# Pooled attention with four experts: a fourth expert's up-projection of the first chunk in seven products instead of eight

## The chip, the cores and the metric

The kernel runs on one core of a Trainium2 chip. A core has a matrix engine (TensorE, PE), a vector engine (VectorE, DVE), a scalar engine (ScalarE, ACT), GpSimd (POOL) and SyncE (SP), each with a queue of its own, and 16 DMA engines. Matrix products are written to PSUM[...]. The metric is the device time of one execution in microseconds (us), as a median of several runs.

## What is computed

Attention over pooled keys and values, and then four experts on every token, weighted by normalized probabilities. Cut to what matters:

```python
# q, k, v: (8 batches, 8 heads, 576 rows, 64)
k_p = k.reshape(B, H, 72, 8, D).mean(axis=3)
v_p = v.reshape(B, H, 72, 8, D).mean(axis=3)
attn = softmax(q @ k_p.T / 8)
x = (attn @ v_p).transpose(0, 2, 1, 3).reshape(4608, 512)
p = probs / (probs.sum(-1, keepdims=True) + 1e-9)      # (4608, 4)
for e in range(4):                                     # w1: 512x1024, w2: 1024x512
    out += p[:, e:e+1] * (relu(x @ w1[e]) @ w2[e])
```

## The kernel before, in words

**Chunks.** The 4608 tokens are worked on as nine chunks of 512: the first 512 rows of each batch (chunks 0 to 7), and the 64 remaining rows of all eight batches together (chunk 8). Each chunk goes through an up-projection (`up`, `up_product`) and a down-projection (`down`, `down_plain`) for each of the four experts. All weights stay in SBUF as bf16. `add` (L825, or L823 for expert 0) multiplies a down product by its probability and adds it to `acc`.

**Seven products.** A projection can be done plainly, or as a 2 x 2 block product with seven block products in place of eight (the Strassen-Winograd scheme). For the plain up-projection, `up` (L596) makes eight blocks of four products with 512 columns (L603), each followed by a relu on ScalarE (L608). For the seven-product one, `up_product` (L663) is called with a step 0 to 6 and a unit 0 or 1 (a unit is half of the hidden columns of each block). Each call makes four products of 256 columns (L681). A unit has two PSUM banks. Step 0 goes into bank 0 and ScalarE copies it into bank 1 (L694). Steps 2 and 3 are copied to the SBUF tile `partial` by ScalarE (L696), steps 1 and 5 end with a relu on ScalarE (L698, L702), and steps 4 and 6 with `relu_sum` on VectorE (L661), which adds a part of `partial`. Beside this the scheme needs sums of blocks: four weight differences for each expert (`first_weight_sums`, L631, the fourth in place in w1), four sums of x for each chunk (`x_sums`, L647), and for the down-projection `weight_sums` (L708) and `hidden_sums` (L721). All of these run on VectorE through `combine` (L245).

**Memory that is shared.** In chunk 0 the partial sums lie in the room of w2 of expert 3 (`partial_first`), so w2 of expert 3 is loaded (`load_w2(3)`, L215) only after their last reader. The x sums of chunk 0 lie in `x_rem`. The keys and values of batch 1 are loaded into `wt_bf`. The hidden rows of experts 0 and 3 of chunk 0 share a buffer.

**PSUM.** Two banks `att`, two banks of unit 1 (`units[1]`), two banks of down chains (`chains`, names `o_ps`), and two banks that are at first `att_first` and later unit 0 (`units[0]`, from the pool `psum_last`). `two_banks(b)` gives attention of batches 0 and 1 `att` and `att_first` in turn.

**The order.** Each engine's order is the program's order, written by hand. `attention_first` makes batch 0's attention and the first expert's up-projection. `first_chunk` (L852) is the rest of chunk 0, with batch 1's attention between its products: expert 1's up-projection plainly, expert 2's by seven products (`both`), expert 3's plainly; expert 0's down-projection by seven products, those of experts 1 and 2 plainly; expert 3's runs in the main loop. Batch 1's queries and keys are transposed on TensorE (`queries`, L356; `keys`, L299) and copied from PSUM by ScalarE or VectorE. `scores` (L374, exponential L385) and `scores_of_two` (exponential L398), `context` (L448), `divide` (L409, L410) and `turn` (L466) follow. Then comes the main loop: for each slot `g` unit 0 makes step `g % 7`, unit 1 makes the step before, and `down` makes a product of the chunk and expert before; a table of slots (`pieces_later`, L948) puts the attention of later batches, their loads and the x sums between the slots. From batch 2 on, transposes are done by DMA from SP's queue: `queries` at L347, `keys` at L293, `turn` at L462, and for the remaining rows of two batches `rem_queries` at L472. `rem_scores` (L485), at slot 6 for batches 0 and 1, reads what L472 delivers; its rows of q come through `load_q_rem` (L197). The loads go through POOL's queue in the order that they are called in.

Of the kernel before, what the change touches and what calls it, by code (L numbers as in the profile page):

```python
# [12 lines left out]
BF16 = mybir.dt.bfloat16  # L13
# [4 lines left out]
def kernel(  # L18
# [10 lines left out]
    nc = tc.nc  # L29
# [230 lines left out]
    def two_banks(b):  # L260
        return att_first[turn_of("att", 2)] if b < 2 else att

# [27 lines left out]
    def keys(b, hs):  # L290
        state[("kpT", b)] = kpTs[b % 3]
        if b >= BUSY:
            nc.sync.dma_start_transpose(  # L293
                out=state[("kpT", b)][:, 0:H], in_=kp_all[:].rearrange("j h a d -> j (h a d)")
            )
            return
        kpt_ps = one_bank(b).bitcast(BF16)[:, 0:H * SP].rearrange("p (h j) -> p h j", j=SP)
        for h in range(hs.start, hs.stop):
            nc.tensor.transpose(kpt_ps[:, h, :], kp_all[0:SP, h], ident[:SP, :SP])  # L299
        copy = nc.scalar.copy if b else nc.vector.tensor_copy  # L300
        copy(out=state[("kpT", b)][:, hs, 0:SP], in_=kpt_ps[:, hs])
# [28 lines left out]

    def open_bank(ps):

        nc.tensor.matmul(ps, lhsT=ident[:], rhs=w1_bf[:, 0, 0, 0:NT], skip_group_check=True)

    def values_folds(b):
# [6 lines left out]
    def queries(b, pair=0):  # L342
# [3 lines left out]
        if b >= BUSY:  # L346
# [4 lines left out]
            return  # L351
        bank = one_bank(b) if b else att_first[pair % 2][:, 0] if pair >= 2 else chains[(pair + 1) % 2][:]
        qt_ps = bank.bitcast(BF16)[:, 0:4 * P].rearrange("p (h a t) -> p h a t", h=2, a=2)
        for hh in range(2):
            for rr in range(2):
                nc.tensor.transpose(  # L356
                    qt_ps[:, hh, rr, :], q_sb[:, 2 * pair + hh, 2 * rr:2 * rr + 2, :], ident[:]
                )
        copy = nc.scalar.copy if pair in ((1, 3), (1, 2))[b] else nc.vector.tensor_copy
        copy(out=state[("qT", b)][:, 2 * pair:2 * pair + 2], in_=qt_ps)  # L360

    def key_columns(b, h, lo):
# [27 lines left out]

    def scores_of_two(b, pair):


        scores(b, pair, 0)
        banks = [unit[1][:] for unit in units]
        score_products(b, pair + 1, banks)
        for r2 in range(2):
            nc.scalar.activation(  # L398
                out=state[("expT", b)][:, 2 * pair + 2:2 * pair + 4, :, r2].rearrange("j h a t -> j (h a) t"),
                in_=banks[r2][0:SP].rearrange("j (h t) -> j h t", t=P),  # L400
                func=ACT.Exp, scale=EXP_SCALE,
            )
# [260 lines left out]
    def up_product(c, e, unit, step):  # L663
        b11, b21, t3, b22 = weight_parts(e)
        a11, _, a12, a22 = x_parts(c)
        t, s, s3 = wu_bf[:, e], state[("xs", c)], third_sum(c)
        banks = units[unit] or [att_first[1][:, i] for i in range(2)]
        bank, grows, lhs, rhs = [
# [183 lines left out]
    def first_chunk():  # L852
# [7 lines left out]

        def both(step):
            for unit in range(2):
                up_product(0, 2, unit, step)

# [6 lines left out]
        each(*sums[1][0:3])  # L871
        up(0, 1, (4,), bank=att_first[1][:, 1])
        each(sums[2][0], sums[2][1], sums[2][3], sums[2][2])
        up(0, 1, (5,), bank=chains[0])
        both(0)
        up(0, 1, (6,), bank=chains[1])
        both(1)
        up(0, 1, (7,), bank=chains[0])
        last_sum = weight_sums(0)
        each(sums[0][3], sums[1][3], *last_sum[0:2])  # L880
        both(2)
        down(0, 0, 0)
        both(3)
        hidden_sums(0, 0, 2)
        down(0, 0, 1)
        both(4)
        hidden_sums(0, 0, 3)
        down(0, 0, 2)
        both(5)
        each(*last_sum[2:])  # L890
        down(0, 0, 3)
        both(6)
        load_w2(3)
        up(0, 3, (0,), bank=units[1][0])
        down(0, 0, 4)
        sums[3][0]()
        fold_keys(1)
        up(0, 3, (1, 2, 3))
        down(0, 0, 5)
        sums[3][1]()  # L900
        down(0, 0, 6)
        up(0, 3, (4,))
        queries(1, 0)
        queries(1, 1)
        sums[3][2]()
        up(0, 3, (5,))
        keys(1, every)
        queries(1, 2)
        up(0, 3, (6,))
        queries(1, 3)  # L910
        up(0, 3, (7,))
        scores(1, 0)
        scores(1, 1)
        each(*weight_sums(1)[0:3])
        down_plain(0, 1, 0)
        fold_first, *fold_rest = values_folds(1)
        fold_first()
        scores(1, 2)
        scores(1, 3)
        each(*fold_rest)  # L920
# [24 lines left out]
        turn(1, 3)  # L945
        each(*(lambda n=n: x_sum(1, n) for n in range(4)))

    def pieces_later():  # L948


        at, amid = {}, {}

# [61 lines left out]
    with tc.manual_schedule(  # L1014
# [14 lines left out]
        load_w1(3)  # L1029
        attention_first()  # L1030
        load_whole(1, k, "kraw")
        load_q(1)
# [3 lines left out]
        first_chunk()  # L1036
        psum_first.__exit__(None, None, None)
        psum_last = ctx.enter_context(
            tc.tile_pool(name="psum_last", bufs=1, space=bass.MemoryType.PSUM))
        units[0] = [psum_last.tile([P, NT], F32, name=f"unit0{i}") for i in range(2)]  # L1040
        open_bank(units[0][1][:])


# [4 lines left out]
        sums = {}  # L1048
        for at, pieces in (((3,), weight_sums(3)[3:]), ((8,), weight_sums(1)[3:]), ((10, 15, 22, 14), weight_sums(2)),
                           ((15,), first_weight_sums(3)[3:])):  # L1050
            for slot, piece in zip(at, pieces, strict=True):
# [57 lines left out]
```

The softmax here doesn't subtract the row's maximum and nothing guards it: scores larger than these inputs give would overflow.

## Time and profile before

| | us |
|---|---|
| median of 4 runs | 491.67 |
| lowest, highest run | 491.49, 492.02 |
| profiled execution | 491.6 |
| its span, first to last instruction | 489.4 |
| TensorE busy in the span | 482.7 |
| VectorE busy | 376.8 |
| ScalarE busy | 304.8 |
| GpSimd busy | 116.5 |

The profile is one execution. Its times count from the span's start. A line of the timeline reads: start, duration, engine, source line, operation, written tile <- read tiles, shapes, number of merged instructions, and in brackets how long the engine stood idle and what ended this. PEld are the weight loads of TensorE, which run beside its products. POOL and SPq lines with DMA are issues; a transfer's landing is told separately, as us from issue to landing. Consecutive instructions on one engine overlap, so the time that an instruction takes of its engine is read from start to start: two `relu_sum`s of 0.69 and 0.68 us start at 40.27 and 40.88. In the stretch of the change the trace has these places: step 6 of expert 2's up-projection starts at 39.53 on TensorE, expert 3's up-projection runs from 40.41 to 51.21 among other work, expert 1's plain down products start at 51.76, chunk 1's first product starts at 66.66.

### The profile page before, as it was taken

Reading aid. Unit: us, or ns where it says so; the run is one execution under the profiler, and the core shown is the slowest. Engines: PE = TensorE matmul, PEld = TensorE weight load, DVE = VectorE, ACT = ScalarE, POOL = GpSimd, SP = SyncE. Lnnn points to the kernel's source line nnn. Section 1 sums busy time; section 2 is a strip of 40 time slices with the busy share of each in tenths; the row PEclk is TensorE's granted clock in tenths of the full one; section 3 lists DMA queues with packets and bytes.
Section 4 is the critical chain, followed back from the end, with each engine's and each line's share of the span. In section 5 each row is a group of like instructions: output and inputs, shape, how many; then the busy total and the mean of one; then the engine's idle time right before and its main releaser. Section 6 shows DMA issues by size and latency. Waiting matters only on the chain.

```text
span 489.4 us, 11551 instructions
## 1 busy us (share of the span) xinstructions
PE 482.7 (99%) x4701; PEld 410.5 (84%) x4701; DVE 376.8 (77%) x758; ACT 304.8 (62%) x580; POOL 116.5 (24%) x115
## 2 busy tenths in 40 slices
PE   8999999999999999999999999999999999999996
PEld 4867468898888888888898888888888888888885
DVE  5778799799768976798679866897678766876674
ACT  5776546855685567657665567556755566556650
POOL 8320323242423055015311452111011101010100
PEclk9999999999999999999999999999999999999999
DMA  9999999995986579544954297311111010004003
GB/s 199 209 208 204 201 165 139 105 85 65 100 118 57 85 81 136 40 79 54 164 49 90 26 160 72 68 23 65 35 23 23 23 66 2 13 21 87 1 1 87
DMA packets 101828, 41.97 MB, mean 86 GB/s; under 512 B 73856, under 2 KB 100224, under 8 KB 101776
## 3 DMA queue, kind: packets, MB, share of 16 engines
q0 software_dynamic: 56944, 22.42, 41.4%
q1 hardware_dynamic: 43728, 17.77, 16.6%
q10 hardware_dynamic: 1104, 1.05, 0.6%
q8 instruction: 37, 0.61, 0.5%
q14 instruction: 15, 0.12, 0.1%
HBM read 45.69 MB, written 9.44 MB: 113 GB/s over the span
## 4 chain that ended last, share of the span: by engine, by line
PE 96%; POOL 1%; DMA 1%; issue 0%; DVE 0%; POOLq 0%
PE o_ps L749 41%; PE unit L681 41%; PE o_ps L775 3%; PE unit L603 2%; PE att L448 1%; PE unit L808 1%; DMA wt_bf<-in_v_dram 1%; PE att L374 1%; PE o_ps L603 1%; POOL wt_bf L141 1%; PE unit L618 1%; PE att_first L681 1%; PE unit L374 0%; PE o_ps L618 0%; PE att L502 0%; PE att L485 0%
## 5 line engine op out<-in xcount | busy, mean ns | idle before, releaser
L825 DVE SCALAR_TENSOR_TENSOR acc<-o_ps,p_all,acc 128x256 f32<-128x256 f32 (+1 forms) x285 | 127.1, 487 | 52.6 <-PE o_ps L749 37.8
L749 PEld LDWEIGHTS <-H 128*128 128x128 bf16 x1320 | 129.1, 98 | 15.2
L681 PEld LDWEIGHTS <-w_bf 128*128 128x128 bf16 x1056 | 102.2, 98 | 12.7 <-issue 0.2
L661 DVE CUSTOM_DVE_ANT_0 H<-unit,partial 128x512 bf16<-128x512 f32 x128 | 87.4, 686 | 26.1 <-ACT partial L696 12.6
L749 PE MATMUL o_ps<-w_bf,H 128*128 128x256 bf16 x792 | 102.6, 273 | 0.0
L681 PE MATMUL unit<-xT,w_bf 128*128 128x256 bf16 x680 | 97.5, 273 | 0.0
L696 ACT COPY partial<-unit 128x512 f32<-128x512 f32 x128 | 72.4, 593 | 29.9 <-PE unit L681 29.9
L763 POOL TENSOR_TENSOR acc<-acc,addend 128x512 f32<-128x512 f32 x24 | 30.4, 1266 | 254.2 <-ACT addend L761 203.1
L681 PEld LDWEIGHTS <-wu_bf 128*128 128x128 bf16 x792 | 75.3, 98 | 11.4 <-issue 2.5
L681 PE MATMUL unit<-xs,wu_bf 128*128 128x256 bf16 x512 | 77.0, 273 | 0.0
L749 PE MATMUL o_ps<-wt_bf,H 128*128 128x256 bf16 x528 | 68.4, 273 | 0.0
L698 ACT ACTIVATE H<-unit 128x512 bf16<-128x512 f32 x64 | 38.9, 607 | 31.5 <-PE unit L681 31.5
L749 PEld LDWEIGHTS <-S 128*128 128x128 bf16 x528 | 51.7, 98 | 6.2
L702 ACT ACTIVATE H<-unit 128x512 bf16<-128x512 f32 x64 | 38.6, 603 | 25.8 <-PE unit L681 25.5
L694 ACT COPY unit<-unit 128x512 f32<-128x512 f32 x65 | 37.9, 584 | 22.0 <-PE unit L681 17.3
L681 PE MATMUL unit<-xs,w_bf 128*128 128x256 bf16 x256 | 38.4, 273 | 0.0
L823 ACT ACTIVATE acc<-o_ps,p_all 128x256 f32<-128x256 f32 x72 | 30.7, 486 | 10.3 <-PE o_ps L749 8.4
L151 POOL DMA_DIRECT2D kraw<-in_k_dram x20 | 26.4, 1320 | 40.7 <-DMA kraw<-in_k_dram 40.7
L681 PE MATMUL unit<-xT,wu_bf 128*128 128x256 bf16 x228 | 34.2, 272 | 0.0
L749 PE MATMUL o_ps<-wt_bf,S 128*128 128x256 bf16 x264 | 34.2, 273 | 0.0
L749 PE MATMUL o_ps<-w_bf,S 128*128 128x256 bf16 x264 | 34.2, 273 | 0.0
L151 POOL DMA_DIRECT2D vraw<-in_v_dram x20 | 29.2, 1462 | 18.5 <-DMA vraw<-in_v_dram 18.5
(170 smaller groups left out, 520.0 us busy)
## 6 DMA issues: line engine op xcount, KB each, us to landing
out_dram<-acc SPq DMA_DIRECT2D x32, 256.0 KB, 4.5
w_bf<-in_moe_w_dram POOLq DMA_DIRECT2D x6, 1024.0 KB, 20.9
q_sb<-in_q_dram POOLq DMA_DIRECT2D x7, 512.0 KB, 9.9
vraw<-in_v_dram POOLq DMA_DIRECT2D x22, 144.0 KB, 6.7
kraw<-in_k_dram POOLq DMA_DIRECT2D x21, 144.0 KB, 6.4
w_bf<-in_moe_w_dram POOLq DMA_DIRECT2D x4, 512.0 KB, 13.7
wt_bf<-in_k_dram POOLq DMA_DIRECT2D x4, 144.0 KB, 5.4
wt_bf<-in_v_dram POOLq DMA_DIRECT2D x4, 144.0 KB, 4.2
```

The costliest lines, as they stand in the source:

```text
L151: nc.gpsimd.dma_start(out=raw[:], in_=rows_of(src, b, 2 * part, 2 * part + 2), accum_op=ALU.add if part else ALU.bypass)
L603: nc.tensor.matmul(out_ps, lhsT=w1_bf[:, e, kc, fc * P:(fc + 1) * P], rhs=xT[:, kc, at], start=(kc == 0), stop=(kc == KC - 1), skip_group_ ...
L661: nc.vector._custom_dve(TENSOR_ADD_SAT, out=dst, in0=ps, in1=part, s0=LARGEST, s1=0.0)
L681: nc.tensor.matmul(ps[:, n * HN:(n + 1) * HN], lhsT=lhs[:, kc, f:f + P], rhs=rhs[:, kc, :], start=(not grows and n == 0 and kc == 0), stop ...
L694: nc.scalar.copy(out=banks[1][:], in_=ps)
L696: nc.scalar.copy(out=part[:, step - 2], in_=ps)
L698: nc.scalar.activation(out=quarter(0, 0), in_=ps, func=ACT.Relu)
L702: nc.scalar.activation(out=quarter(0, 1), in_=ps, func=ACT.Relu)
L749: nc.tensor.matmul(ps[:, j], lhsT=lhs[:, i, j * P:(j + 1) * P], rhs=rhs[:, i, :], start=(not grows and i == 0 and j == 0), stop=(i == HF - 1),
L763: nc.gpsimd.tensor_add(out=dst, in0=dst, in1=addend[:])
L823: nc.scalar.activation(out=dst, in_=o_ps, func=ACT.Copy, scale=prob)
L825: nc.vector.scalar_tensor_tensor(out=dst, in0=o_ps, scalar=prob, in1=dst, op0=ALU.mult, op1=ALU.add,)
```

## The change

Expert 3's up-projection in chunk 0 is made by `up_product`, like expert 2's. Its four weight differences are made in `first_chunk`; the fourth was at slot 15 of the main loop before. In `both`, expert 3 goes unit 1 first. `load_w2(3)` moves behind its last step, because the partial sums now lie in that room until then. The pool `psum_first` is closed, and unit 0's own banks are opened, before `first_chunk` instead of after it, so that the bank-opening product (`open_bank`, L333) is left out. Batch 1's attention now has `att` alone: its queries are transposed in two groups of four heads (`queries_of_two`), the keys go to a bank of `chains`, and its scores are made by `scores_of_two` with bank 0 of both units as the second pair of banks. One x sum of chunk 1 moves to slot 0 of the main loop. The diff, with the removal of `open_bank` itself left out:

```diff
@@ -258,7 +258,7 @@
         return units[1][turn_of("work", 2)][:]
 
     def two_banks(b):
-        return att_first[turn_of("att", 2)] if b < 2 else att
+        return att if b else att_first[turn_of("att", 2)]
 
     def one_bank(b):
         return spare_bank() if b == 0 else two_banks(b)[:, 0]
@@ -294,7 +294,7 @@
                 out=state[("kpT", b)][:, 0:H], in_=kp_all[:].rearrange("j h a d -> j (h a d)")
             )
             return
-        kpt_ps = one_bank(b).bitcast(BF16)[:, 0:H * SP].rearrange("p (h j) -> p h j", j=SP)
+        kpt_ps = (chains[1][:] if b else spare_bank()).bitcast(BF16)[:, 0:H * SP].rearrange("p (h j) -> p h j", j=SP)
         for h in range(hs.start, hs.stop):
             nc.tensor.transpose(kpt_ps[:, h, :], kp_all[0:SP, h], ident[:SP, :SP])
         copy = nc.scalar.copy if b else nc.vector.tensor_copy
@@ -349,15 +345,28 @@
                 in_=q_sb[:].rearrange("p h r d -> p (h r d)"),
             )
             return
-        bank = one_bank(b) if b else att_first[pair % 2][:, 0] if pair >= 2 else chains[(pair + 1) % 2][:]
+        bank = att_first[pair % 2][:, 0] if pair >= 2 else chains[(pair + 1) % 2][:]
         qt_ps = bank.bitcast(BF16)[:, 0:4 * P].rearrange("p (h a t) -> p h a t", h=2, a=2)
         for hh in range(2):
             for rr in range(2):
                 nc.tensor.transpose(
                     qt_ps[:, hh, rr, :], q_sb[:, 2 * pair + hh, 2 * rr:2 * rr + 2, :], ident[:]
                 )
-        copy = nc.scalar.copy if pair in ((1, 3), (1, 2))[b] else nc.vector.tensor_copy
+        copy = nc.scalar.copy if pair % 2 else nc.vector.tensor_copy
         copy(out=state[("qT", b)][:, 2 * pair:2 * pair + 2], in_=qt_ps)
+
+    def queries_of_two(pair, bank, copy):
+
+        q_sb = raws[("q", 1)]
+        if pair == 0:
+            state[("qT", 1)] = apool.tile([P, H, 2, P], BF16, name="qT")
+        qt_ps = bank.bitcast(BF16)[:, 0:8 * P].rearrange("p (h a t) -> p h a t", h=4, a=2)
+        for hh in range(4):
+            for rr in range(2):
+                nc.tensor.transpose(
+                    qt_ps[:, hh, rr, :], q_sb[:, 2 * pair + hh, 2 * rr:2 * rr + 2, :], ident[:]
+                )
+        copy(out=state[("qT", 1)][:, 2 * pair:2 * pair + 4], in_=qt_ps)
 
     def key_columns(b, h, lo):
 
@@ -388,11 +397,12 @@
             func=ACT.Exp, scale=EXP_SCALE,
         )
 
-    def scores_of_two(b, pair):
-
-
-        scores(b, pair, 0)
-        banks = [unit[1][:] for unit in units]
+    def scores_of_two(b, pair, bank=1):
+
+
+
+        scores(b, pair, 0 if b > 1 else None)
+        banks = [unit[bank][:] for unit in units]
         score_products(b, pair + 1, banks)
         for r2 in range(2):
             nc.scalar.activation(
@@ -664,7 +674,7 @@
         b11, b21, t3, b22 = weight_parts(e)
         a11, _, a12, a22 = x_parts(c)
         t, s, s3 = wu_bf[:, e], state[("xs", c)], third_sum(c)
-        banks = units[unit] or [att_first[1][:, i] for i in range(2)]
+        banks = units[unit]
         bank, grows, lhs, rhs = [
             (0, False, b11, a11),
             (1, True, b21, a12),
@@ -858,9 +868,9 @@
 
         sums = {e: first_weight_sums(e) for e in range(E)}
 
-        def both(step):
-            for unit in range(2):
-                up_product(0, 2, unit, step)
+        def both(e, step):
+            for unit in (1, 0) if e == 3 else (0, 1):
+                up_product(0, e, unit, step)
 
         each(*(lambda n=n: x_sum(0, n) for n in range(4)), *sums[0][0:3])
         norm_probs()
@@ -869,54 +879,50 @@
         hidden_sums(0, 0, 1)
         up(0, 1, (2, 3))
         each(*sums[1][0:3])
-        up(0, 1, (4,), bank=att_first[1][:, 1])
+        up(0, 1, (4,), bank=units[0][1][:])
         each(sums[2][0], sums[2][1], sums[2][3], sums[2][2])
         up(0, 1, (5,), bank=chains[0])
-        both(0)
+        both(2, 0)
         up(0, 1, (6,), bank=chains[1])
-        both(1)
+        both(2, 1)
         up(0, 1, (7,), bank=chains[0])
         last_sum = weight_sums(0)
         each(sums[0][3], sums[1][3], *last_sum[0:2])
-        both(2)
+        both(2, 2)
         down(0, 0, 0)
-        both(3)
+        both(2, 3)
         hidden_sums(0, 0, 2)
         down(0, 0, 1)
-        both(4)
+        both(2, 4)
         hidden_sums(0, 0, 3)
         down(0, 0, 2)
-        both(5)
+        both(2, 5)
         each(*last_sum[2:])
         down(0, 0, 3)
-        both(6)
+        both(2, 6)
+        each(*sums[3][0:2])
+        both(3, 0)
+        down(0, 0, 4)
+        both(3, 1)
+        each(sums[3][3], sums[3][2])
+        fold_keys(1)
+        down(0, 0, 5)
+        both(3, 2)
+        down(0, 0, 6)
+        both(3, 3)
+        queries_of_two(0, att[:, 0], nc.scalar.copy)
+        both(3, 4)
+        both(3, 5)
+        keys(1, every)
+        queries_of_two(2, chains[0][:], nc.vector.tensor_copy)
+        both(3, 6)
         load_w2(3)
-        up(0, 3, (0,), bank=units[1][0])
-        down(0, 0, 4)
-        sums[3][0]()
-        fold_keys(1)
-        up(0, 3, (1, 2, 3))
-        down(0, 0, 5)
-        sums[3][1]()
-        down(0, 0, 6)
-        up(0, 3, (4,))
-        queries(1, 0)
-        queries(1, 1)
-        sums[3][2]()
-        up(0, 3, (5,))
-        keys(1, every)
-        queries(1, 2)
-        up(0, 3, (6,))
-        queries(1, 3)
-        up(0, 3, (7,))
-        scores(1, 0)
-        scores(1, 1)
+        scores_of_two(1, 0, 0)
         each(*weight_sums(1)[0:3])
         down_plain(0, 1, 0)
         fold_first, *fold_rest = values_folds(1)
         fold_first()
-        scores(1, 2)
-        scores(1, 3)
+        scores_of_two(1, 2, 0)
         each(*fold_rest)
         load_wide(0, 0)
         load_q(2)
@@ -943,12 +949,12 @@
         each(*weight_sums(3)[0:3])
         down_plain(0, 2, 2)
         turn(1, 3)
-        each(*(lambda n=n: x_sum(1, n) for n in range(4)))
+        each(*(lambda n=n: x_sum(1, n) for n in range(3)))
 
     def pieces_later():
 
 
-        at, amid = {}, {}
+        at, amid = {0: [lambda: x_sum(1, 3)]}, {}
 
         def put_amid(slot, piece):
             amid[slot] = piece
@@ -1028,26 +1034,23 @@
         load_w2(0)
         load_w1(3)
         attention_first()
+        psum_first.__exit__(None, None, None)
+        psum_last = ctx.enter_context(
+            tc.tile_pool(name="psum_last", bufs=1, space=bass.MemoryType.PSUM))
+        units[0] = [psum_last.tile([P, NT], F32, name=f"unit0{i}") for i in range(2)]
         load_whole(1, k, "kraw")
         load_q(1)
         load_w2(1)
         load_whole(1, v, "vraw")
         load_w2(2)
         first_chunk()
-        psum_first.__exit__(None, None, None)
-        psum_last = ctx.enter_context(
-            tc.tile_pool(name="psum_last", bufs=1, space=bass.MemoryType.PSUM))
-        units[0] = [psum_last.tile([P, NT], F32, name=f"unit0{i}") for i in range(2)]
-        open_bank(units[0][1][:])
-
 
 
         N = len(order)
         later, amid = pieces_later()
         below_of = [(0, 3)] + order
         sums = {}
-        for at, pieces in (((3,), weight_sums(3)[3:]), ((8,), weight_sums(1)[3:]), ((10, 15, 22, 14), weight_sums(2)),
-                           ((15,), first_weight_sums(3)[3:])):
+        for at, pieces in (((3,), weight_sums(3)[3:]), ((8,), weight_sums(1)[3:]), ((10, 15, 22, 14), weight_sums(2))):
             for slot, piece in zip(at, pieces, strict=True):
                 sums.setdefault(slot, []).append(piece)
         POOLED = (4,)
```

More of the change, by code (lines that the diff above doesn't have):

```diff
@@ L329, in idle @@
             nc.tensor.matmul(w_ps[:, 0:cols], lhsT=zeros[:, 0:P], rhs=zeros[:, 0:cols])
-    def open_bank(ps):
-        nc.tensor.matmul(ps, lhsT=ident[:], rhs=w1_bf[:, 0, 0, 0:NT], skip_group_check=True)
     def values_folds(b):
```

## The prediction

> **What bounds the kernel now.** I read the page's busy shares first, then its slices, the waits of TensorE, the groups and windows of the stretch that the change rewrites, and last the transfers around it.
>
> ```profile
> PE 482.7 (99%) x4701; PEld 410.5 (84%) x4701; DVE 376.8 (77%) x758; ACT 304.8 (62%) x580; POOL 116.5 (24%) x115
> PE   8999999999999999999999999999999999999996
> DMA  9999999995986579544954297311111010004003
> PE 96%; POOL 1%; DMA 1%; issue 0%; DVE 0%; POOLq 0%
> ```
>
> TensorE is busy in every slice and is 96% of the chain that ended last, so removed TensorE time is a gain only if TensorE then waits for nothing. The DMA engines are full for the first nine slices (9 x 12.2 = 110 us, though by bytes only until about 73 us). The waits of TensorE in the whole span come to 2 us, all before 13 us:
>
> ```profile
> PE unit L329 <- DVE H L844: 1.3, 1, 1.3
> PE att_first L528 <- DVE kpT L301: 0.4, 1, 0.4
> PE unit L309 <- DMA wt_bf<-in_v_dram: 0.3, 1, 0.3
> ```
>
> The stretch itself by windows (us, then busy time of PE, PEld, DVE, ACT, POOL):
>
> ```profile
> 40.27:57.00 16.73, 16.73 (x121) 9.31 (x120) 13.30 (x23) 11.08 (x18) 0.88 (x1) 1.00 1.27 205
> 57.00:69.00 12.00, 12.00 (x99) 6.74 (x98) 10.93 (x21) 2.92 (x5) 5.59 (x7) 1.00 1.44 187
> 69.00:79.50 10.50, 10.47 (x96) 9.23 (x95) 10.19 (x21) 6.37 (x12) 2.23 (x2) 1.00 1.14 126
> ```
>
> VectorE has only 16.73 - 13.30 = 3.4 us free in the stretch that gets its new work, and DMA runs at about 200 GB/s. The last rows are a transfer that TensorE meets later (timeline; then issues with us to landing):
>
> ```profile
> 73.20 1.20 SPq L472 DMA_TRANSPOSE qTr<-q_rem  x1
> 79.40 0.39 PEld L485 LDWEIGHTS <-kpT 64*128 64x128 bf16 x16 [0.21 <-issue]
> 79.50 0.41 PE L485 MATMUL att<-qTr,kpT 64*128 64x64 bf16 x16
> ...
> qTr<-q_rem SPq DMA_TRANSPOSE x1, 6.3
> ```
>
> 73.20 + 6.3 = 79.5: the transposed queries of the remainder rows land when TensorE needs them. The weight loads stand ready at 79.40, the products start at 79.50. The list of waits does not name this, because it is short; it is the place where I expect the gain to go.
>
> [...]eight 256-column products of L749 take 36.91 to 37.78, 0.87 us (109 ns each); four 512-column ones of L603 0.866 us (217 ns). [...]the DVE rows here stand in the program's order, so a late piece delays all behind it. [...]on the POOL queue w2 of expert 2 (issued 28.91, 29.0 to landing) lands at 57.95, w2 of expert 3 (issued 42.09, 21.5) at 63.6: 5.7 us for its 1 MB after 15 us of standing in line.
>
> **The change part by part.**
>
> *TensorE.* Up-projection 3 was 8 x 4 = 32 products of 512 columns, 32 x 0.2165 = 6.93 us. It becomes 2 units x 7 x 4 = 56 of 256 columns, 56 x 0.1088 = 6.09: 0.84 less. The bank-opening product of L333 goes: 66.45 to 66.66, 0.21. Transposes of queries and keys, score products and their two visits keep their number. Together 1.05 us.
>
> *VectorE.* Added: four relu sums (steps 4 and 6, two units), 4 x 0.61 = 2.44 (L661 rows start 40.27 and 40.88). The fourth weight difference moves here from slot 15: 0.61 (starts 38.59, 39.20). Two query copies of 512 (0.41) become one of 1024: between 0.67 (576 to 512 elements cost little more, L301 and L360) and 0.82 (twice 0.41); I take 0.67, so -0.15. Sum +2.9, against 3.4 free, but each idle piece can be filled only if work is ready.
>
> *ScalarE.* Eight relus (8 x 0.60) become ten evictions (2 per unit at steps 0, 1, 2, 3, 5; 0.47 start to start), one copy of 1024 (two of 0.59, so 1.0 to 1.2) replaces two, two exponentials of 1024 become four of 512: about +1.2 us against 16.73 - 11.08 = 5.6 free. I find no place where it is last, apart from the first one below.
>
> *The queues added up.* I lay the new program order out from TensorE's 39.53 (first product of step 6, expert 2), which doesn't move, with the durations above, 0.2 us from a product's issue end to its reader and 0.06 us between other engines. The same addition for the order of before gives 51.74, 57.58 and 66.62 for the first plain down product, the first context and chunk 1's first product; the trace has 51.76, 57.60, 66.66.
> - Step 0 for expert 3 starts at 40.4 with unit 1. Its copy into the other bank waits for the relu sums of expert 2, which VectorE does as unit 0, unit 1 (end 41.56). Step 1 wants both copies from 42.13: TensorE waits 0.09.
> - VectorE: differences 0 and 1 to 42.8, the add of down step 4 to 43.6, differences 3 and 2 to 44.8, key folds 2.7 to 47.5, add of step 5 to 48.2, relu sums of step 4 to 49.5, query copy 49.6, relu sums of step 6 to 51.5, three w2 differences of expert 1 to 53.6, add of the first plain product 54.2, value folds and pooled values to 56.6, add of the second plain product 56.6 to 57.3.
> - TensorE meets each in time (difference 1 wanted at 43.9; relu sums of step 4 at 49.4 and 49.9; keys at 48.7; pooled values at 56.76 against 56.7) until the fourth plain product of expert 1, due at 57.0: its bank is read by the add that ends at 57.34. Wait 0.38. Before, that add stood at the same time (56.67) but TensorE came at 57.86. So VectorE, full from 40.3 to 57.3, takes back a third.
> - One buffer for batch 1's contexts costs nothing: a context is divided 0.9 us after its products, plus up to 0.7 behind an add, and the next comes 2.2 us later (59.59, 61.80 in the trace). This is covered by the plain down product of 1.73; without it the next would follow at 60.07 and wait until 61.44, 1.4 each.
> - Wait that goes: 0.05 at the fourth query transpose.
> So TensorE enters chunk 1 at 1.05 + 0.05 - 0.09 - 0.38 = 0.63 us earlier.
>
> *Moved load.* w2 of expert 3 shares memory with the partial sums, so it is issued after the last relu sum, at 51.6 instead of 42.1. On POOL nothing stands behind it until 57.05 (load for batch 2, which waits for the pooled values). [...]it loses 9.5 us of standing in line and still lands at 63.6; VectorE wants it at 65.3. Cost zero with 57.95 - 52.5 = 5.4 us of cover.
>
> *Moved pieces.* One x sum (0.34) goes behind an add in slot 0; it is first read at step 6, 10 us later. VectorE loses 0.61 at slot 15. Neither is waited for.
>
> *What is late next.* TensorE comes to the remainder scores at 79.40 - 0.63 = 78.77. Their queries come by a chain that the change doesn't touch: POOL queue full to 73.13 (q_rem issued 61.93, 11.2 to landing), transposed from 73.20, landing 79.46. Nothing earlier on SP waits for TensorE: before it stands only the batch-2 query transpose, which also follows a load. So TensorE waits 0.73 and goes on at 79.50 as before. From there both kernels have the same work.
>
> **Sum.** 1.05 + 0.05 - 0.47 - 0.63 = 0.0 against the profiled execution, 491.6 (span 489.4 and 2.2 around it); that lies 0.07 under the median of 491.67. I predict **491.6**. About 0.2% (1 us) is what can be told from no change.
>
> **Rivals.**
> 1. *The wait takes all* (forecast, 0.62): 491.6. For it: 79.46 against 79.50. Since 0.63 disappears there, errors in my queue sum up to that size do not show.
> 2. *The transfer comes earlier* (0.18). The transpose took 6.3 us where a later one of the same size took 2.5, beside a value load (issued 72.27, 7.0 to landing) and an output store. If that overlap shifts by 0.7 us, the gain of 0.63 to 1.05 stays: 491.0 to 490.5, half of it beyond the bound.
> 3. *VectorE is longer* (0.12). If its full queue from 40.3 to 57.3 runs over my sum by more than the 0.73 of wait in hand, each us more is one of loss: a 1.0 us copy, or relu sums that wait for ScalarE, give 492 to 493.
> 4. *The moved load loses its place in line* (0.08). It decides at 57.95: if its descriptors aren't ready by then, it and all loads behind it (q_rem too) slip by the delay. If it kept its 21.5 us from issue it would land at 74.0, VectorE would stand from 65.3 with adds behind, TensorE some 8 us: 499.
> That seven products aren't fewer columns is excluded by the counts above.
>
> **Numbers.** Beyond 0.2% faster: half of rival 2, 0.09. Slower: 0.09 of rival 3 and 0.08 of rival 4, 0.17. Within: 0.74. Range 490.7 (rival 2) to 492.6 (rival 3).
>
> **What would show it.** Right: 56 products more on L681; VectorE without gaps from 40 to 57; a wait of 0.3 to 0.5 at the fourth plain product of expert 1; chunk 1's first product near 66.0; w2 of expert 3 landing near 63.6; a wait of about 0.7 for qTr near 78.8 and products at 79.5. Wrong: qTr landing before 79, or chunk 1 starting after 66.7.

## The result, and the profile after

Before: 491.58 us (median of 63, 490.9 to 492.61). After: **493.07 us** (median of 43, 490.96 to 495.36). Ratio 1.0034, 95% interval 1.0027 to 1.0041: slower by about 0.3%, beyond the 0.2% that can be told from no change. The forecast was 491.6, and its range ended at 492.6. The profiled execution after took 494.18, with a span of 492.3.

Each execution is listed with its span as well. The rest, time minus span, is a median 2.2 in the kernel before and 1.9 in the changed one and four of the experiments on it; in the other kernels below it lies between 1.9 and 2.4. What sets it isn't shown. The forecast took 2.2 for both kernels, so differences below are given by the span too where they rest on less than a microsecond: the median span is 489.4 before (of the 67 executions taken along with the first experiments), and 491.25 after.

The first lines of the page after, as those shown of before (1: busy time; 2: the slices):

```profile
PE 483.7 (98%) x4724; PEld 413.7 (84%) x4724; DVE 379.0 (77%) x761; ACT 305.5 (62%) x583; POOL 116.4 (24%) x115
PE   8999998999999999999999999999999999999996
PEclk9999998999999999999999999999999999999999
```

23 products more, and yet 1.0 us *more* of TensorE's time (482.7 to 483.7), though the new products are cheaper by count. The page says where to look: in the seventh slice (74 to 86 us) TensorE's busy share and its granted clock both fall to 8. The waits of TensorE after (us in total, times, longest) have two lines that before had not, the first and the last:

```profile
PE att L495 <- DMA qTr<-q_rem: 1.9, 1, 1.9
PE unit L329 <- DVE H L854: 1.3, 1, 1.3
PE att_first L538 <- DVE kpT L301: 0.4, 1, 0.4
PE o_ps L785 <- DVE acc L835: 0.2, 1, 0.2
```

The last one is the wait for VectorE at the fourth plain product that the prediction put at 0.38 (0.2 in the list, 0.32 by the starts of the products around it). The first is the wait for the queries of the remainder rows, at the predicted place, but 1.9 us instead of 0.73. (L681, L485 and L472 of before are L691, L495 and L482 here.) The timeline after (start, us, engine, line):

```profile
51.87 0.88 POOL L215 DMA_DIRECT2D w_bf<-in_moe_w_dram  x1 [22.11 <-ACT expT L394]
...
65.83 0.60 PE L691 MATMUL unit<-xT,w_bf 128*128 128x256 bf16 x4
...
74.06 1.19 SPq L482 DMA_TRANSPOSE qTr<-q_rem  x1
...
78.56 0.09 PEld L495 LDWEIGHTS <-kpT 64*128 64x128 bf16 x1 [0.21 <-issue]
80.55 0.41 PE L495 MATMUL att<-qTr,kpT 64*128 64x64 bf16 x16 [1.91 <-DMA qTr<-q_rem]
```

Chunk 1 starts at 65.83 (before 66.66), TensorE stands ready for the remainder scores at 78.56 (forecast 78.77), and waits to 80.55 (before 79.50). So TensorE is early as forecast, and *the transfer is late by 1.05*. The DMA issues after (KB each, us from issue to landing) trace it back:

```profile
w_bf<-in_moe_w_dram POOLq DMA_DIRECT2D x1, 1024.0 KB, 13.2
...
qTr<-q_rem SPq DMA_TRANSPOSE x1, 6.4
```

w2 of expert 3 lands at 51.87 + 13.19 = 65.06 where it landed at 63.6, and VectorE begins to read it at 65.11; the remainder's queries, behind it on the POOL queue, follow, and their transposition is issued at 74.06 instead of 73.20 and takes 6.4 as before (6.3). The windows around the pause show a second loss (stretch, length, busy us with instructions of PE, PEld, DVE, ACT, POOL, granted clock, DMA share, GB/s):

```profile
78.56:80.55 1.99, 0.08 (x2) 0.09 (x1) 1.69 (x4) 0.00 (x0) 1.99 (x3) 1.00 1.20 227
80.55:82.00 1.45, 1.45 (x27) 1.29 (x27) 0.03 (x1) 1.00 (x2) 1.45 (x3) 1.00 1.16 240
82.00:85.30 3.30, 3.30 (x18) 2.31 (x16) 2.48 (x5) 1.21 (x4) 0.24 (x1) 0.50 1.30 165
85.30:88.00 2.70, 2.70 (x38) 2.18 (x37) 1.51 (x4) 1.85 (x4) 1.42 (x1) 0.98 1.45 210
```

From 82.0 to 85.4 TensorE is "busy" all the time, but at clock 0.50: 18 products in 3.30 us. Eight products of 256 columns take 1.70 there (83.25 to 84.95), and 0.87 at full clock (37.55 to 38.42), 0.109 each. In the trace the half clock lasts 3.413 us (82.01 to 85.43), so it costs 3.413 / 2 = 1.7. A busy share can't show this; the clock column does. The lists of executions give each one's mean clock: in 19 of 44 of the changed kernel (the 43 and the profiled one) it is 0.996 or less, and these take 493.79 or more (median 494.2); the other 25, called undisturbed below, take 490.96 to 493.75 (median 492.6, span 490.7). 3.413 us at half clock in 492 lowers the mean by 0.0035, so 0.996 is its mark.

My theory, then: w2 of expert 3, issued 10 us later, lets the POOL queue run partly dry; everything behind it lands about 1 us late; TensorE pauses for 2 us, and the pause now and then costs it a stretch of half clock. Rivals: VectorE's or chunk 1's new order is what costs; or the half clock is unrelated to the pause.

### The profile page after: what moved, and what is told of

Same layout as the page of the kernel before. It is cut to its first block, busy times and chain, and to the rows that moved or that the text cites. A ratio compares the mean times of both kernels' runs of the same rounds, so it can differ in the third digit from the quotient of the medians.

```text
span 492.3 us, 11604 instructions
## 1 busy us (share of the span) xinstructions
PE 483.7 (98%) x4724; PEld 413.7 (84%) x4724; DVE 379.0 (77%) x761; ACT 305.5 (62%) x583; POOL 116.4 (24%) x115
## 3 DMA queue, kind: packets, MB, share of 16 engines
q10 hardware_dynamic: 1104, 1.05, 0.6%
## 4 chain that ended last, share of the span: by engine, by line
PE 83%; DMA 12%; POOL 3%; DVE 1%; issue 0%; POOLq 0%; SPq 0%
PE unit L691 39%; PE o_ps L759 39%; DMA wt_bf<-in_v_dram 6%; DMA w_bf<-in_moe_w_dram 3%; DMA q_rem<-in_q_dram 3%; PE att L458 1%; DMA qTr<-q_rem 1%; PE unit L818 1%; POOL wt_bf L141 1%; PE att L383 1%; PE unit L383 0%; DVE wt_bf L270 0%; PE o_ps L785 0%; PE att L512 0%; POOL w_bf L206 0%
## 5 line engine op out<-in xcount | busy, mean ns | idle before, releaser
L691 PEld LDWEIGHTS <-w_bf 128*128 128x128 bf16 x1088 | 105.6, 98 | 13.4 <-issue 0.2
L691 PE MATMUL unit<-xT,w_bf 128*128 128x256 bf16 x704 | 101.3, 274 | 0.0
L691 PEld LDWEIGHTS <-wu_bf 128*128 128x128 bf16 x816 | 77.6, 98 | 11.6 <-issue 2.5
L691 PE MATMUL unit<-xs,wu_bf 128*128 128x256 bf16 x512 | 77.0, 273 | 0.0
L708 ACT ACTIVATE H<-unit 128x512 bf16<-128x512 f32 x66 | 39.9, 607 | 32.7 <-PE unit L691 32.7
L712 ACT ACTIVATE H<-unit 128x512 bf16<-128x512 f32 x66 | 39.7, 603 | 25.8 <-PE unit L691 25.5
L704 ACT COPY unit<-unit 128x512 f32<-128x512 f32 x68 | 39.5, 584 | 23.0 <-PE unit L691 17.5
L691 PE MATMUL unit<-xs,w_bf 128*128 128x256 bf16 x256 | 38.4, 273 | 0.0
L691 PE MATMUL unit<-xT,wu_bf 128*128 128x256 bf16 x240 | 35.7, 272 | 0.0
L151 POOL DMA_DIRECT2D vraw<-in_v_dram x20 | 27.9, 1396 | 25.3 <-DMA vraw<-in_v_dram 21.7
```

The source lines that it names most:

```text
L151: nc.gpsimd.dma_start(out=raw[:], in_=rows_of(src, b, 2 * part, 2 * part + 2), accum_op=ALU.add if part else ALU.bypass)
L691: nc.tensor.matmul(ps[:, n * HN:(n + 1) * HN], lhsT=lhs[:, kc, f:f + P], rhs=rhs[:, kc, :], start=(not grows and n == 0 and kc == 0), stop ...
L704: nc.scalar.copy(out=banks[1][:], in_=ps)
L708: nc.scalar.activation(out=quarter(0, 0), in_=ps, func=ACT.Relu)
L712: nc.scalar.activation(out=quarter(0, 1), in_=ps, func=ACT.Relu)
```

## The experiments

Times are medians with lowest and highest, ratios are against executions of the kernel before that were taken along with them. "At half clock" means a mean clock of 0.996 or less.

**Fill the pause.** Nine products of loaded data into a bank that is free there, ahead of the first remainder scores:

```
+        for _ in range(9 if i == 0 else 0):
+            nc.tensor.matmul(att[:, 0], lhsT=ident[:], rhs=w1_bf[:, 0, 0, 0:NT], skip_group_check=True)
```

> The changed kernel, with nine extra 512-column products into the attention bank just ahead of the first remainder scores, so that TensorE works for about 1.9 us where it stood idle for 2.0. Their result is overwritten. Theory (the pause of TensorE itself halves its clock for some 3.3 us and costs 1.6 us): the half-speed stretch at 82 to 85 us goes, the wait for qTr shrinks to 0.1 us or so, its landing stays near 80.5, and the time is 492.4 with a narrow spread. Rival (the half-speed stretch has another cause[...]): still there, time near 493 to 494.

492.67 (492.11 to 494.55), ratio 1.0022 [1.0015, 1.0029]. Its timeline and its window:

```profile
78.22 2.10 PE L492 MATMUL att<-w_bf,ident 128*128 128x512 bf16 x9
80.68 0.41 PE L497 MATMUL att<-qTr,kpT 64*128 64x64 bf16 x16 [0.35 <-DMA qTr<-q_rem]
```

```profile
82.00:85.30 3.30, 3.30 (x44) 2.77 (x43) 2.89 (x6) 2.28 (x5) 0.22 (x1) 1.00 1.26 162
```

The queries are as late as before (80.68 against 80.55), but TensorE is busy almost until then, and the clock stays at 1.00. Over all executions, 1 of 21 has a mean clock of 0.996 or less, instead of 19 of 44. So at this place the pause does bring the half clock. Without it the change still loses: 492.67 is at the 492.6 of the undisturbed 25. (The filler itself takes 9 x 0.2165 = 1.95 us, also where the queries come earlier, so this is no measure of the wait alone.)

**Put the remainder scores later**, so that TensorE comes after the queries:

```
-            ... rem=(0, 6, 8, 14),
+            ... rem=(0, 8, 11, 14),
```

> The changed kernel, with the first remainder scores at slot 8 instead of 6 and their context at slot 11 instead of 8, so that qTr has 3.5 us more. Theory (the wait for qTr is the only place where the change loses): no wait, no half-speed stretch, TensorE keeps its 0.83 us of lead and loses the 0.1 us that the kernel before waited too: 490.7. Rival (something else after 66 us holds TensorE, for example VectorE): between 491.2 and 493.

491.36 (490.87 to 492.2), ratio 0.9991 [0.998, 1.0002], no execution at half clock. The wait for the queries is gone (products at 81.70), and with it 1.7 of the after time. Less came back than expected. A part of the difference is a new wait; the timeline of this kernel around 104 us:

```profile
103.47 0.69 DVE L420 TENSOR_TENSOR x_tok<-att,inv 128x512 bf16<-128x512 f32 x1
...
104.22 0.42 PE L458 MATMUL att<-vp,expT 72*128 72x65 bf16 x8
```

The context at slot 16 now comes right behind a remainder's, and its products begin when VectorE has divided the last one, 0.23 late. The rest of the miss, some 0.4, I didn't find.

**Only the late load, in the kernel before.** The load is moved as far as in the change, behind a GpSimd addition that reads the last weight sums; nothing else is changed:

```
-        load_w2(3)
...
+        late = wt_bf[:, 1, 0, 0, 0:HN]
+        nc.gpsimd.tensor_add(out=addend[:, 0], in0=late, in1=late)
+        load_w2(3)
```

> The kernel before, with w2 of expert 3 issued at about 52 us as in the changed kernel, behind a small GpSimd addition that reads a VectorE result of that time; nothing else differs. Theory (the late issue leaves a hole in the load queue): qTr lands about 0.8 to 1.0 us later, near 80.4, TensorE waits about 1 us, time 492.3 or more. Rival (the later landing in the changed kernel is the spread of the loads): qTr near 79.5, time 491.6.

492.36 (491.33 to 496.97), ratio 1.0031 [1.0016, 1.0046]; 4 of 22 executions at half clock, against 1 of 67 of the kernel before. Issued at 52.24; the scores in its trace wait 0.89, longer than in the first trace of before, but little longer than the 0.73 in its second trace further down; the queries land at 79.86, where 80.4 was expected:

```profile
79.90 0.41 PE L485 MATMUL att<-qTr,kpT 64*128 64x64 bf16 x16 [0.89 <-DMA qTr<-q_rem]
```

So the late issue alone, without the seven products, costs 0.76 in time, of which 0.55 in the span (489.95 against 489.4); the other 0.2 lies outside the span. The four at half clock take 495.64 to 496.97, 3.4 or more over the median of the rest (492.26), where one such stretch costs 1.7: what else they lose isn't shown. Nor does the one trace show the 0.55 at the queries alone: its execution took 493.17, and behind TensorE's last product its span goes on for 5.5 us, in before for 4.5.

**The change with the load where it was.** The partial sums of expert 3 get other room (buffers that chunk 1 fills later), so that its w2 needs to wait for nobody:

```
+        if c == 0 and e == 3:
+            part = rooms()[unit]
...
         both(2, 6)
+        load_w2(3)
...
         both(3, 6)
-        load_w2(3)
```

> The changed kernel, with the partial sums of expert 3 in rooms that are free at that time (the next x block, the next x sums, the addend), so that w2 of expert 3 is issued near 42 us as before. Theory: w2 of expert 3 lands near 63.6 and qTr near 79.5, TensorE waits about 0.9 us, time 491.6, the forecast on record. Rival (spread of the loads, or another piece of the change delays them): qTr near 80.5 and 492.5 to 494.

491.37 (490.35 to 494.08), ratio 0.9997 [0.9988, 1.0005]; 1 of 21 at half clock. By the span this is the forecast, no change (489.5 against 489.4), and the 0.2 under 491.6 lies outside the span. It comes about by the forecast's mechanism, a wait for the queries that takes the gain of chunk 0 back:

```profile
78.60 0.41 PE L495 MATMUL att<-qTr,kpT 64*128 64x64 bf16 x16 [0.33 <-DMA qTr<-q_rem]
```

So neither VectorE's added work nor the new order around chunk 1 makes the kernel slower; the rival that says so falls. (The wait is shorter than the 0.73 of the forecast in this one trace, whose execution took 490.55.)

**The same, with the load late again** (issued at 51.78, behind a GpSimd addition that reads the last relu sum):

```
+        late = H_bufs[0][:, 1, 0, 2, :]
+        nc.gpsimd.tensor_add(out=addend[:, 1], in0=late, in1=late)
+        load_w2(3)
```

> As the run with early w2 (changed kernel, partial sums of expert 3 in other rooms), but w2 of expert 3 is issued near 51.8 us, behind a small GpSimd addition that reads a relu sum. Theory (the time of issue alone delays the loads): the DMA rate falls near 53 to 55 us, qTr lands at 80 to 80.6 and the time goes from 491.4 to 492.4 or more. Rival (the rooms, that is writing partial sums into w2's memory, or something else in the changed kernel makes the loads late): 491.4, qTr near 79.

492.19 (491.38 to 494.88), ratio 1.0013 [1.0, 1.0027]; 2 of 13 at half clock. Against the early one that is +0.82, and late against early in the kernel before is +0.76 (492.36 - 491.6). By the span it is 0.6 here (490.1 against 489.5) and 0.55 there. In this kernel's trace w2 of expert 3 lands at 51.78 + 12.9 = 64.68, against 41.55 + 22.7 = 64.25 with the early load, the queries land at 79.27, and TensorE waits 0.4 for them. So the expectation is met in part: the time of issue alone costs something, but less than expected, and the queries are nearer to the rival's 79 than to 80.

This leaves a part of the loss open. In the change itself, late against early is 1.2 in the span even in the undisturbed executions (490.7 against 489.5), twice what the moved issue alone shows, and half clock comes in 19 of 44 instead of 2 of 13. The late run differs from the change in the rooms of the partial sums and in the GpSimd addition. The rival that names the rooms, writing partial sums into w2's memory, isn't excluded for the other half.

Ten traces show how far the load moves the queries. Their transposition is issued at 72.96 to 73.39 in the four with the early load and at 73.50 to 74.25 in the six with the late one, on average 0.66 later; they land on average at 79.3 and 80.0. This is about the size of the 0.55 and 0.6.

Now the windows of a load that is issued 6 us before 57.95, where its predecessor lands in before, and still loses. Of each kernel the stretches 53 to 56 and 58 to 62, the last number is GB/s; before (early):

```profile
53.00:56.00 3.00, 3.00 (x21) 1.31 (x19) 2.27 (x3) 2.66 (x3) 0.00 (x0) 1.00 1.24 207
58.00:62.00 4.00, 4.00 (x36) 2.15 (x34) 3.51 (x7) 0.59 (x1) 4.00 (x6) 1.00 1.23 193
```

after (late):

```profile
53.00:56.00 3.00, 3.00 (x18) 1.33 (x15) 2.94 (x4) 1.99 (x3) 0.00 (x0) 1.00 1.21 187
58.00:62.00 4.00, 4.00 (x39) 2.37 (x38) 3.40 (x6) 0.72 (x2) 4.00 (x6) 1.00 1.17 171
```

the changed kernel with the early load:

```profile
53.00:56.00 3.00, 3.00 (x17) 1.35 (x16) 2.93 (x5) 1.82 (x3) 0.00 (x0) 1.00 1.24 207
58.00:62.00 4.00, 4.00 (x40) 2.35 (x39) 3.43 (x8) 1.09 (x2) 4.00 (x6) 1.00 1.25 198
```

the kernel before with the late load:

```profile
53.00:56.00 3.00, 3.00 (x20) 1.41 (x20) 2.69 (x4) 2.21 (x3) 0.16 (x1) 1.00 1.15 177
58.00:62.00 4.00, 4.00 (x39) 2.34 (x38) 3.51 (x8) 0.59 (x1) 4.00 (x6) 1.00 1.20 192
```

Between 53 and 56 the rate goes with the issue: over all 14 traces of the study it is 207 or 208 in the seven with the early load and 177 to 187 in the seven with the late one. An issue as such doesn't lower the rate: about 2 to 5 us after the early one it is 206 to 212 in the seven traces, in before

```profile
44.00:47.00 3.00, 3.00 (x24) 2.15 (x22) 2.93 (x6) 1.52 (x3) 0.00 (x0) 1.00 1.25 208
```

20 to 30 GB/s over 3 us are 60 to 90 KB, 0.3 to 0.45 us of transfer at 200 GB/s. The load ahead, w2 of expert 2, lands later as well in the trace after: at 28.85 + 30.6 = 59.45; why isn't shown. That the POOL queue runs partly dry from about 53 on is my estimate from this rate. No view here shows single engines, or what stands in a queue.

What the windows don't settle: in the changed kernel the late load has a second low stretch (58 to 62: 171 and 169 against 198) and lands at 64.68 to 65.46 in five traces; in the kernel before it has none (192 against 193) and lands at 63.82 and 64.11.

**Both corrections**: the early load, and the first remainder scores one slot later (`rem=(0, 7, 8, 14)`).

> The changed kernel with the partial sums of expert 3 in free rooms, so that w2 of expert 3 is issued near 42 us, and the first remainder scores at slot 7 instead of 6 (their context stays at slot 8). Theory (the change gives 0.77 us in chunk 0, and the wait for qTr is what takes it back): no wait for qTr, 491.6 - 0.77 - 0.1 = 490.7, faster than both kernels. Rival (another wait takes the place, as in the run with slot 8, where a context waited 0.2 us): 491.2 to 491.5.

**490.36** (489.95 to 491.73), ratio 0.9977 [0.9969, 0.9985]: faster than both kernels, no execution at half clock. Its waits of TensorE are only the two that before had as well, and its scores start unhindered:

```profile
PE unit L329 <- DVE H L865: 1.3, 1, 1.3
PE att_first L538 <- DVE kpT L301: 0.4, 1, 0.4
```

```profile
79.94 0.41 PE L495 MATMUL att<-qTr,kpT 64*128 64x64 bf16 x16
```

The gain of chunk 0 is kept, because nothing waits for the queries. 491.72 - 490.36 = 1.36 is more than that gain of 0.6 to 0.8: 0.36 of it lies outside the span, and of the 1.0 in the span (489.5 to 488.5) the part beyond the gain can be the wait of the kernel before, which has it too in other executions. The next pair shows it.

**Both kernels once more**, unchanged, for a second trace of each.

> The kernel before once more, for a second trace of its loads. Theory: w2 of expert 2 lands near 58.0, w2 of expert 3 near 63.6 to 64.2, qTr between 78.5 and 79.7, DMA rate flat from 48 to 57 us. Rival (loads vary by more than 1 us from execution to execution): w2 of expert 3 near 65.

> The changed kernel once more, for a second trace. Theory: a hole in the DMA rate near 53 to 55 us, w2 of expert 3 near 65.0, qTr near 80.5, a wait of about 2 us, with or without a stretch of half clock after it. Rival (the first trace was an outlier): qTr near 79.5 and a wait of about 1 us.

491.96 and 491.09, one execution each. Before waits for the queries after all:

```profile
79.86 0.41 PE L485 MATMUL att<-qTr,kpT 64*128 64x64 bf16 x16 [0.73 <-DMA qTr<-q_rem]
```

After misses its expectation of a wait near 2 us: w2 of expert 3 lands at 65.46, late as expected, but the transposition is issued 0.4 earlier than in the first trace (73.66) and takes 5.4 instead of 6.4, TensorE stands ready 0.3 later (chunk 0 took 33.89 from expert 2's first row product instead of 33.52), and the wait is 0.2; the time is near the lower end of the 44. So single executions differ by 0.3 to 1.0 in each of these quantities, and what holds is the medians.

**Does a pause anywhere halve the clock?** For this the wait for the queries had to go first: in these four kernels, all from the kernel before, every transposing transfer is a plain one of the same bytes, so keys, queries and x of the later batches aren't transposed and the values aren't attention.

```
-            nc.sync.dma_start_transpose(
+            nc.sync.dma_start(
```

> A base for the next three: the kernel before with each of its DMA transposes replaced by a plain DMA of the same bytes, so that the transposition of keys, queries and x from batch 2 on is left out and the values there are not attention. Both theories: qTr lands about 2 us after q_rem, near 75 to 76, no wait for it, 491.0 to 491.6.

491.22 (490.88 to 492.15), ratio 0.9995 [0.9986, 1.0003]. The queries land at 75.1, long before TensorE. On this base a pause of chosen length, at slot 108: a GpSimd addition of 32 columns that waits for the sums, and a product that waits for it; then the same with 512 columns:

```
+            if g == 108:
+                pause = addend[:].rearrange("p j d -> p (j d)").bitcast(BF16)[:, 0:32]
+                nc.gpsimd.tensor_add(out=pause, in0=acc[:, 0, NT - 32:NT], in1=acc[:, 0, NT - 32:NT])
+                nc.tensor.matmul(att[:, 0, 0:32], lhsT=ident[:], rhs=pause, skip_group_check=True)
```

> The base without transposition, with one made pause of TensorE late in the main loop (slot 108, near 260 us): a 32-column product that reads a 32-column GpSimd addition of an accumulator row that VectorE has just written; its result is overwritten. A pause of about 1 to 1.3 us. Theory (a pause of 1 us leaves the clock alone, one of 2 us can halve it): the base and 1.2 us, no half-speed stretch. Rival (any pause of about 1 us halves the clock): the base and 2.8 us, with a stretch of doubled product pitch.

> The same with 512 columns, so that the pause is 2 to 2.5 us. Theory: the base and 2.3 us in the executions that keep their clock, and 1.6 us more in those that have a half-speed stretch of some 3.3 us after the pause, about half of each. Rival (the half clock of the changed kernel belongs to its place near 80 us and not to the pause): the base and 2.3 us in all.

Short: 492.22 (491.84 to 493.2), ratio 1.0014 [1.0006, 1.0021], a pause of 1.2 in the trace. Long: 493.41 (492.71 to 493.97), ratio 1.0027 [1.0002, 1.0052], a pause of 2.0 (1.76 of idleness and the added product). Its row, and the window behind it:

```profile
271.01 0.38 PE L1079 MATMUL att<-addend,ident 128*128 128x512 bf16 x1 [1.76 <-POOL addend L1078]
```

```profile
271.00:275.00 4.00, 3.99 (x36) 3.48 (x36) 2.45 (x6) 1.20 (x3) 0.00 (x0) 1.00 0.01 4
```

A pause nearly as long as the one of after (1.76 idle against 1.91), and the clock stays at 1.00 behind it; none of the 6 executions is at half clock, and they cost about what the pause is long (493.41 - 491.22 = 2.2). That is what the rival, the place near 80 us, expected. The clock records of the traces offer another reason.

They change on a grid: in all 14 traces each full-clock stretch is a whole multiple of 3.413 us long (141 or 142 windows of this length; in before 481.28 us, 141 windows; in after 75.09 us, 22 windows, then 406.19, 119), from a start that differs from trace to trace (3.96 to 6.92 us; 5.87 in before, 6.92 in after). Counted in windows of this grid (length, then TensorE's busy us; the clock is the third number from the end), after's pause falls into one window, and the made pause is split between two. Third, the end of before, where TensorE runs out of work:

```profile
78.60:82.01 3.41, 1.50 (x28) 1.35 (x28) 1.68 (x5) 1.01 (x2) 3.41 (x5) 1.00 1.19 234
82.01:85.42 3.41, 3.41 (x19) 2.35 (x17) 2.59 (x5) 1.32 (x4) 0.23 (x1) 0.50 1.30 165
```

```profile
267.35:270.76 3.41, 1.91 (x18) 1.56 (x16) 2.35 (x5) 1.10 (x3) 0.84 (x1) 1.00 0.21 62
270.76:274.17 3.41, 3.16 (x28) 2.73 (x28) 1.62 (x4) 1.15 (x2) 0.20 (x1) 1.00 0.02 5
```

```profile
483.73:487.14 3.41, 1.21 (x12) 0.84 (x9) 1.34 (x3) 0.00 (x0) 0.00 (x0) 1.00 0.70 177
487.14:489.40 2.26, 0.00 (x0) 0.00 (x0) 0.00 (x0) 0.00 (x0) 0.00 (x0) 0.50 0.29 82
```

In these 14 traces the clock halves at the end of the first window in which TensorE is busy for 0.44 of it (after's pause) or less (at the end of the kernel: 0.06 to 0.41 in six traces, 0.35 in before; not at all in the other eight, after among them). It stays full after every window with 0.49 or more; the made pause leaves 0.56 and 0.93. One window with 0.44, at the end of the trace with the short pause, kept it too, so 0.44 was seen on both sides; the ends of products are modelled, so the shares are rough. 0.44 of a window leaves 1.9 us of idleness. So, as an estimate from these numbers, the made pause of 1.76 was too short wherever it fell on the grid, and one of 1.9 to 2.0 halves the clock only if it falls almost whole into one window, which is luck, a little under one time in two. That would give a number like 19 of 44; how long the other executions waited isn't recorded. Whether the place matters beside this was not tried.

**The late load on this base**, where TensorE meets no query transfer:

> The base without transposition, with w2 of expert 3 issued at about 51.7 us, the moment of the changed kernel, behind a 32-column GpSimd addition. The loads up to 69 us are those of the kernel before. Theory [...]: rate falls near 53 to 55 us, w2 of expert 3 lands near 64.7 to 65.2 and the last q_rem at 73.5 to 74. Rival (lateness alone does little, and the changed kernel adds something of its own): w2 of expert 3 near 63.8, last q_rem near 73.2.

491.46 (491.02 to 492.12), ratio 0.9994 [0.9983, 1.0005], within the plain one's interval. The rate between 53 and 56 falls to 184 as in the other late ones, and the time doesn't follow: the late load costs where TensorE waits for the remainder's queries, and nothing that can be told from noise where it doesn't. In this pair's traces w2 of expert 3 lands at 64.11 both times, so it says nothing on the landing.

## Why the prediction was wrong

**The gain of chunk 0: right.** From the up-projection of expert 2 (its first row product, 32.54 before, 32.31 after) to chunk 1's first product it is 34.12 before and 33.52 after, so 0.60 (forecast 0.63); in four of the experiments on the changed order 33.34 or 33.35, so 0.77, in the fifth 0.66, and in the second trace after only 0.23. VectorE was full as added up: 16.16 of 16.73 us busy (forecast 13.3 + 2.9 = 16.2), and the wait at the fourth plain product is 0.32 by its pitch, 0.2 to 0.4 in the other traces of this order (forecast 0.38). The spacing of products is the same after: eight of 256 columns take 0.87 (37.55 to 38.42), four of 512 take 0.86 (29.71 to 30.57), so the sum stands.

**Where the gain goes: right.** TensorE gives it back at the remainder scores, and with the load left early (491.37) or with the scores later as well (490.36) the forecast mechanism shows both ways. Rival 2 shows in single executions: in the second trace after the transposition takes 5.4, and the time is 491.09.

**"*Moved load* ... it loses 9.5 us of standing in line and still lands at 63.6 ... Cost zero with 57.95 - 52.5 = 5.4 us of cover": the failing step.** The last landing of the load ahead was taken for the time to which the whole queue is full. The rate falls from 53 on (187 GB/s against 207 between 53 and 56), the load lands at 65.06, and the transposition of the queries, which stand behind it, is issued 0.66 later on average. Cost 0.55 and 0.6 in the span from the moved issue alone (two pairs; 0.8 in time), not zero, and 1.2 in the change itself without half clock; the reason for the other half is open. The 65.3 at which VectorE was to want the load stands in no line: VectorE reads it at 65.72 before and at 65.11 after, right behind its landing, and TensorE is not held up by that. Rival 4 named such a slip of the load and of all behind it, but with the same wrong point of decision (57.95) and a price of 8 us for a delay that was about 1. That nothing earlier on SP waits for TensorE was right and didn't help: the chain that I called untouched by the change begins behind the moved load.

**A term that the sum lacks: the clock.** I priced a wait by its length. In 19 of 44 executions the longer one brought 3.4 us of half clock, 494.2 - 492.6 = 1.6 in time (1.7 by the trace). The trace after has it behind a window of 3.413 us with TensorE busy for 1.50 of it (0.44).

**A term taken as fixed: the 2.2 around the span.** It is 1.9 in the changed kernel, 0.3 in its favour, which no part of the forecast foresaw. It hides a part of the loss.

**The sum by the measured terms**: 491.6 + 1.3 (span of the undisturbed, 490.7 against 489.4) - 0.3 (outside the span) + 1.6 x 19 / 44 (clock, 0.7) = 493.3, against a median of 493.07. Of the 1.3, about 0.6 is shown for the moved issue, 0.1 is the early kernel's own difference from before, and about 0.6 is open.

**Open.** Why the late load costs twice as much in the changed kernel as in the two pairs, and why it loses a second stretch (58 to 62) in the changed kernel's traces only. How little work in a window halves the clock (0.44 did once and once did not): pauses moved by fractions of a window at one place were not tried. Whether the queries, loaded ahead of batch 2's loads, would save the wait with the load left late was not measured.

## What to carry to other kernels

The landing of a long transfer didn't tell here how late the next one may be issued at no cost: with the next one issued at 51.6 to 52.2 us, 6 us before the landing of before (57.95), the rate between 53 and 56 was 177 to 187 GB/s instead of 207. Read the rate by windows, and issue the next transfer ahead of its fall. When buffers are shared to save room, ask what the later release does to the transfer that refills them and to all that is queued behind it. Price a wait of about 2 us on TensorE by its length and, beside it, by one window of half clock with a chance (here 1.7 us, in 19 of 44 executions).

## What was unexpected of the hardware

- A rate of 207 GB/s falls to 177 to 187 between 53 and 56 us, 5 us before the load in hand lands in before (57.95), if the next one is issued at 51.6 to 52.2 instead of 41.6 to 42.3 (seven traces each).
- Full-clock stretches that are whole multiples of 3.413 us (141 in before, 22 and 119 in after), and half clock for one such window after one that TensorE was busy for 0.44 of; 19 of 44 executions are at half clock, 1 of 21 with the pause filled, and none of 6 with a made pause of 1.76 us.
- The transposition of the remainder's queries varies between 5.4 and 6.7 us in traces of kernels that issue it alike; as a plain transfer it takes 2.0 to 2.3.
